# Attention followed by a squared-ReLU MLP on one core: the transpose of one token tile moves from TensorE to a DMA, and the order around it is planned anew

## The chip, the cores and the metric

The kernel runs on one core of one Trainium2 chip. The metric is the device time of one execution in microseconds (us). The kernel before takes 211.44 us, the median of 4 runs (211.15 to 211.97). Smaller is better.

## What is computed

The inputs are q, k and v of shape (4, 8, 768, 64) in float32 (batch, heads, sequence, head size), and two weight matrices, `w_in` (512 x 2048) and `w_out` (2048 x 512). Cut to its core, the reference is:

```
scores = (q @ k.T) / 8 + bias            # per batch and head; bias = -slope[h] * distance
scores = where(keep, scores, -1e9)       # keep: 96 local positions back, and the 8 first ones
a   = softmax(scores)
x   = (a @ v), heads side by side        # 3072 tokens x 512
h   = max(x @ w_in, 0)
out = (h * h) @ w_out                    # 3072 tokens x 512
```

Because only the last 96 positions and the first 8 count, a tile of 128 queries needs the keys and values of its own tile and of the tile before it, plus 8 global positions.

## The kernel before, in words

**Tiles and blocks.** The 3072 tokens are 24 tiles of 128, six to a batch. Two tiles make a block (12 blocks) for the MLP, so tiles 6 and 7 are block 3, tiles 8 and 9 block 4, and so on. Tile 0, 6, 12 and 18 are the first of a batch and have no tile to their left.

**What one tile goes through.** Each step is an operation with a short name; `sc(9)` is the scores of tile 9, `s1(3,0)` the first slice of the first MLP matmul of block 3.

- `load(j)`: POOL starts three DMAs, for q, k and v of the tile, which also turn float32 into bf16 (line 213, called from line 244). q and k go into one of three shared buffers (`qk_6` to `qk_8`), so a load waits until the transposes of the tile three places earlier have read that buffer.
- `T(j)`: q and k are transposed. Tiles 0 to 5 do it on TensorE (`tr`, line 402) with a copy out of PSUM; from tile 6 on (`JQK = 6`) SP starts one transposing DMA (line 426).
- `gate(j)` for tiles 8, 9, 10 (line 376): a tiny DVE write into the q/k buffer, placed in DVE's order so that the load that follows it cannot start before that point.
- `sc(j)`: score matmuls on TensorE into PSUM (line 489); `exp` on ACT (line 555); `mul` by a table of exp(bias) and mask on DVE (line 580).
- `pv(j,0)`, `pv(j,1)`: probabilities times v for four heads each (line 642, tile `po`); `norm` on DVE: a reciprocal (line 669) and a multiplication (line 670) that writes half of `x` of the tile.
- `x` (128 tokens x 512) must be transposed to `xT` before the MLP can use it. For tiles under `JX` TensorE does it: `trx` (line 705), four 128x128 transposes into PSUM, and a copy to SBUF, on ACT (line 330) or DVE (line 332), whichever the planner takes. For tiles from `JX` on, SP starts a transposing DMA (line 729) and nothing else is needed. Before, `JX = 8`.
- `gk`, `gv`, `kl`: small DVE copies that put the 8 global keys and values next to the tile for its right neighbour.

**What one block goes through.** `s1(b,s)`, s = 0 to 7: eight matmuls `xT` x `w_in` into PSUM (line 757, tile `hT`); `relu` on ACT (line 778, `hr`); `sq` on DVE (line 790, `hs`); `s2(b,s,half)`: two matmuls `hs` x `w_out` each for tile 0 and 1 of the block (line 830, `acc`); after the eighth slice `o` copies `acc` to SBUF (ACT or DVE) and `st` stores it (SP, line 872).

**What sets the order.** A planner (class `Plan`) is run when the kernel is built. It holds for each operation its engine, a cost, what it depends on, and a due key; it emits the instructions of every engine in the order in which its model starts them, and on the chip each engine runs its list strictly in that order. The key of tile j's operations comes from `LEADS` (line 178: how much ahead of its block a tile is due) and from `SHIFT` (line 34: a correction for each kind of operation, or for one kind and one tile or block). `STEP` (line 188) ties `sc(j)` behind a certain `s1`; `HOLD` (line 187) lets the next `s1` also wait for that `sc`. `SAFE` and `SAFEX` (lines 179, 180) add time to the model's landing of some transposing DMAs. `JOIN` puts the scores of a tile into one operation with those of the tile before.

**Shared resources.** Six PSUM banks (tag `g`) go round among `tr`, `sc`, `po`, `trx` and `hT`; two belong to `acc`. `xT` has three buffers, `x` two, `hr` two, `hs` fourteen. SP's list holds all transposing DMAs (of q/k and of x) and all stores, in one order; POOL's list holds all loads.

Of the kernel before, what the change touches and what calls it, by code (L numbers as in the profile page):

```python
# [21 lines left out]
class Plan:  # L22
# [8 lines left out]

    LAG = {"PE": 0.25, "ACT": 0.26, "DVE": 0.2, "SP": 0.6, "POOLQ": 0.8, "DMAQ": 1.2, "DMA": 0.0}
    URGE = 0.01
    SHIFT = {'T': 47, 'sc': -5.25, 'pv': -2, 'norm': 26.5, 'trx': -2, 'xT': 51, 'gk': 42, 'gv': -127.5, 'mul': 24, 'kl': 38.5, 'relu': 25.5, 'sq': 30, 's2': -5, 'o': 61, 'st': 78, ('mul', 3): 28, ('tr', 4): 10, ('xT', 5): -22, ('sc', 6): 14, ('pv', 7): -4, ('norm', 7): -17, ('trx', 7): -3, ('sc', 8): -12, ('pv', 8): -18, ('pv', 10): 45, ('sc', 11): 12, ('pv', 12): -50, ('sc', 13): 17, ('sc', 14): 6, ('pv', 14): 10, ('norm', 14): -28, ('sc', 15): -21, ('exp', 15): 20, ('exp', 16): 83, ('mul', 16): 92, ('norm', 16): -9, ('sc', 17): 32, ('pv', 17): 28, ('pv', 21): 9.5, ('pv', 22): -10, ('norm', 22): 8, ('s1', 2): -8.5, ('sq', 2): -10, ('relu', 3): 24, ('sq', 3): -82, ('s1', 5): 6, ('s1', 6): 30, ('sq', 6): 6, ('s1', 7): -6, ('sq', 7): -92, ('relu', 8): 40, ('s1', 9): -2, ('s1', 10): -10, ('s2', 0): 7.5, ('s2', 2): 1, ('s2', 4): -15, ('s2', 5): 37, ('s2', 6): -5, ('s2', 7): -3, ('s2', 9): 4.5, ('s2', 11): 30}

    def shift(self, name):
        early = name[-1 if name[0] in ("T", "tr") else 1]
        return self.SHIFT.get(name[0], 0.0) + self.SHIFT.get((name[0], early), 0.0)

# [65 lines left out]
def kernel(  # L105
# [35 lines left out]
    NFIRST = 4  # L141
    NSPLIT = 4
    NBIAS = 3
    JQK, JX = 6, 8
    NQ, NKT = 3, 2 * TPB
    NG = 8 - NACC
    G = ("g", NG)
# [7 lines left out]
    def const(shape, dt, name):  # L155
        return consts.tile(shape, dt, name=name, tag=name)
# [18 lines left out]
    pbt = const([P, 2, P], FP32, "pbt")  # L175
    pbw = const([P, 2, P], FP32, "pbw")
    plan = Plan()
    LEADS = {3: 51, 4: 17, 5: 16, 6: 27, 8: 2, 9: 20, 10: 42, 11: 47, 12: 0, 14: 0, 15: 7.5, 16: 34, 17: 46, 20: 28, 21: 15, 23: 56}
    SAFE = {j: 1.6 for j in range(6, 12)} | {14: 4.2, 15: 3.2, 16: 3.5}
    SAFEX = {9: 1.5, 11: 1.5, 13: 2.5}  # L180

# [2 lines left out]
    JOIN = {(7, 0), (12, 0), (21, 0), (16, 0), (23, 0), (18, 0), (20, 0), (15, 0)}  # L184
    COPY = [14, 15, 19, 20, 22]
    BEHIND = {}
    HOLD = ((10, 0),)
    STEP = {(4, 0): -7, (12, 0): 37, (5, 0): -2, (10, 0): 29, (13, 0): 30, (23, 1): 81}
    JGATE = 11
    NHS = 14  # L190
    NWARM = 8
# [72 lines left out]
    def emit_ones(e, js):  # L264
        for j in js:
            nc.vector.memset(v_sb[j][:, :, D : D + 1], 1.0)
# [38 lines left out]
    for g in range(NFIRST + 2, NT, 6):  # L305
        js = range(g, min(g + 6, NT))
        o = plan.op(
            ("ones", g), {"DVE": 0.2}, lambda e, js=js: emit_ones(e, js),
            key=-1.0, ready=15.0,
        )  # L310
# [40 lines left out]
    kl = [const([P, NPAIR, P], BF16, f"kl_{i}") for i in range(2 if COPY else 0)]  # L351
# [8 lines left out]
    for j in range(NT):  # L360
        b, t = divmod(j, TPB)
        first = t == 0
        need = 8 * (j // 2)
        base = need - LEADS.get(j, LEAD) + 4 * (j % 2)
        if (j, 0) in JOIN:
# [29 lines left out]
        for n in range(2) if j < JQK else ():  # L395
            users = []

            def emit_tr(e, j=j, n=n, fp=fp):
# [9 lines left out]
            tr = plan.op(  # L408
                ("tr", n, j), {"PE": 0.5 if fp else 0.24}, emit_tr,
                deps=[land["qk"[n], j]], key=base, takes=(*G, [users]),  # L410
            )
# [12 lines left out]
        if j >= JQK:  # L424
            def emit_dT(e, j=j, T_=T_):
# [5 lines left out]
            T = plan.op(  # L431
                ("T", j), {"SP": 1.3}, emit_dT,
                deps=[land["q", j], land["k", j], xT_op[j - 3]] + ku, key=base - 6,
            )
            T = plan.op(("moved", j), {"DMAQ": 1.2}, None, deps=[T])
            qk_users[slot(j)].append(T)
            if j in SAFE:

                T = plan.op(("seen", j), {"DMA": SAFE[j]}, None, deps=[T])
# [6 lines left out]
        mul, mul_users = {}, {}  # L446
# [55 lines left out]
        for gs in SETS.get(j, [tuple(range(groups))]):  # L502
            n = 8 * len(gs)
            sc_users = busers[2 * gs[0] : 2 * gs[-1] + 2]
            if (j, gs[0]) in JOIN:

                o, also, taken = joint
# [16 lines left out]
            if j < NBIAS:  # L524
# [6 lines left out]
            o = plan.op(  # L531
                ("sc", j, gs[0]), {"PE": 0.2 + 0.029 * n},
                lambda e, gs=also, f=emit_sc: f(e, gs), deps=[*deps, bias],
                key=base + 1 + 2 * gs[0], takes=takes,
            )
# [91 lines left out]
        norm = []  # L627
# [170 lines left out]
    for o in plan.ops:  # L798
        if o["name"][0] == "sc":
            j = o["name"][1]  # L800
            n = STEP.get(o["name"][1:], 4 * j - LEAD)
            if n >= 0 and j >= NFIRST:
                o["deps"].append(s1_ops[n // NSTEP, n % NSTEP])
                if o["name"][1:] in HOLD:
                    n += 1
                    s1_ops[n // NSTEP, n % NSTEP]["deps"].append(o)

    for blk in range(NBLK):
# [9 lines left out]
        for s, sub, half in order2:  # L818
# [5 lines left out]
            def emit_s2(e, blk=blk, s=s, sub=sub, half=half, w=w, cols=cols, own=own):  # L824
# [15 lines left out]
            o = plan.op(  # L840
                ("s2", blk, s, sub), {"PE": 0.43 * w / d_model}, emit_s2,
                deps=[d, land["wout", s]] + users[-1:],
                key=8 * blk + s + 2.0 + (0 if not last else 8 * sub + 8 * (half or 0)),
                takes=((*G, [users]) if own else ("acc", NACC, [users])) if s == 0 else None,
            )
# [6 lines left out]
            if s == NSTEP - 1:  # L852
# [14 lines left out]
                def emit_st(e, blk=blk, sub=sub, half=half, cols=cols):  # L867
# [9 lines left out]
                st = plan.op(  # L877
                    ("st", blk, sub), {"SP": 0.8 if (blk, sub) in HALVES else 0.4}, emit_st,
                    deps=[ev, s1_ops[NLATE, 0] if blk < NLATE - 2 else None],
                    key=8 * blk + s + 9.0,  # L880
                )
                st = plan.op(("stored", blk, sub), {"DMAQ": 1.4}, None, deps=[st])
# [40 lines left out]
```

## Time and profile before

| | |
|---|---|
| median of the 4 runs | 211.44 us |
| the profiled execution | 211.66 us |
| its span, first to last instruction | 209.9 us |
| TensorE (PE) busy | 202.5 us, 96% of the span |
| DVE, ACT, POOL busy | 140.9, 120.0, 73.8 us |
| chain that ended last | PE 88%, POOL 5%, DMA 4% |
| `hT` matmuls, L757 | x768 |
| `acc` matmuls, L830 | x373 |
| `trx` transposes, L705 | x32 |
| transposing DMAs of x, L729 | x16 |
| transposing DMAs of q/k, L426 | x18 |

The profile is of one execution. Its own time is 211.66 us, 1.76 us more than its span and 0.22 us over the median of the runs. A group's line gives how many instructions it has, the busy time and the mean of one in ns, and the idle time of the engine just before them. PE is the matmul stream, PEld the loads of its weights, which run beside it. "DMA to landing" is the time from the start of the issue on the queue to the arrival of the data. The stretch up to about 20 us is the start, in which TensorE waits for the first slices of `w_in`; the last 10 us are the second matmul of the last block, its copy and its store.

### The profile page before, as it was taken

How to read it: one execution, taken by the hardware profiler on the slowest of the kernel's cores; microseconds unless marked ns; L12 is line 12 of the kernel's file. 1: busy time of each engine (PE TensorE's matmuls, PEld its weight loads, DVE VectorE, ACT ScalarE, POOL GpSimd, SP SyncE). 2: the span in 40 equal slices, each digit the busy share in tenths (PEclk: the TensorE clock that was granted, in tenths of full speed). 3: DMA queues.
4: the chain of work that ended last, by engine and by line, in shares of the span. 5: the costliest groups of instructions: out<-in, count | busy, mean ns of one | idle time of the engine just before them, and what ended most of it. 6: DMA issues, size and time to landing. Idle time of an engine off the chain costs nothing.

```text
span 209.9 us, 4980 instructions
## 1 busy us (share of the span) xinstructions
PE 202.5 (96%) x1957; PEld 141.8 (68%) x1984; DVE 140.9 (67%) x370; ACT 120.0 (57%) x224; POOL 73.8 (35%) x91
## 2 busy tenths in 40 slices
PE   7997999999999999999999999999999999999994
PEld 3776877666756677676866676776676865865853
DVE  7698698533595878585968666676696865781730
ACT  6785678234772674664737464663575826841631
POOL 8996766431927064413274222222500000000000
PEclk9999999999999999999999999999999999999999
DMA  9999999999999999999999692989983421130402
GB/s 131 152 168 186 184 190 199 177 176 213 139 169 119 196 139 134 213 91 95 214 152 144 177 102 52 133 127 142 197 61 75 123 55 28 54 96 3 102 0 100
DMA packets 112649, 27.32 MB, mean 130 GB/s; under 512 B 103282, under 2 KB 109682, under 8 KB 112626
## 3 DMA queue, kind: packets, MB, share of 16 engines
q0 software_dynamic: 79200, 13.37, 83.9%
q1 hardware_dynamic: 33426, 13.64, 33.1%
q8 instruction: 15, 0.25, 0.5%
q14 instruction: 8, 0.07, 0.1%
HBM read 27.26 MB, written 6.29 MB: 160 GB/s over the span
## 4 chain that ended last, share of the span: by engine, by line
PE 88%; POOL 5%; DMA 4%; issue 1%; DVE 1%; ACT 0%; POOLq 0%
PE acc L830 39%; PE hT L757 39%; PE sc L489 5%; PE po L642 4%; DMA win<-in_moe_w_in_dram 4%; POOL qk L213 3%; POOL v L213 2%; POOL win L213 1%; PE trx L705 1%; PE tr L402 1%; DVE x L670 0%; DVE hs L790 0%; POOL pbi L269 0%; DVE rs L669 0%; ACT o L330 0%
## 5 line engine op out<-in xcount | busy, mean ns | idle before, releaser
L757 PE MATMUL hT<-xT,win 128*128 128x256 bf16 x768 | 93.5, 273 | 1.4 <-DMA win<-in_moe_w_in_dram 1.3
L830 PE MATMUL acc<-wout,hs 128*128 128x512 bf16 (+2 forms) x373 | 87.1, 370 | 1.7 <-issue 0.3
L778 ACT ACTIVATE hr<-hT 128x512 f32<-128x512 f32 x96 | 57.3, 603 | 47.5 <-PE hT L757 42.3
L757 PEld LDWEIGHTS <-win 128*128 128x128 bf16 x768 | 72.8, 98 | 15.7 <-DMA win<-in_moe_w_in_dram 1.9
L790 DVE TENSOR_TENSOR hs<-hr 128x512 bf16<-128x512 f32 x96 | 64.7, 686 | 23.5 <-ACT hr L778 22.8
L830 PEld LDWEIGHTS <-hs 128*128 128x128 bf16 x400 | 36.8, 98 | 33.8
L555 ACT ACTIVATE esc<-sc 128x512 bf16<-128x512 f32 x78 | 39.9, 613 | 12.6 <-PE sc L489 12.6
L213 POOL DMA_DIRECT2D qk<-in_q_dram x23 | 20.6, 898 | 70.1 <-DMA qkT<-qk 54.3
L580 DVE TENSOR_TENSOR at<-esc,E 128x512 bf16<-128x512 bf16 x78 | 32.3, 422 | 10.1 <-ACT esc L555 7.2
L330 ACT COPY o<-acc 128x512 f32<-128x512 f32 (+2 forms) x21 | 11.6, 576 | 19.8 <-PE acc L830 19.8
L213 POOL DMA_DIRECT2D v<-in_v_dram x24 | 21.8, 909 | 2.0 <-DMA win<-in_moe_w_in_dram 1.6
L670 DVE TENSOR_TENSOR x<-po,rs 128x256 bf16<-128x256 f32 x48 | 20.4, 424 | 1.7
L213 POOL DMA_DIRECT2D qk<-in_k_dram x23 | 20.8, 907 | 0.5 <-DMA win<-in_moe_w_in_dram 0.5
L642 PEld LDWEIGHTS <-at 128*128 128x128 bf16 x352 | 15.7, 98 | 4.5
L642 PE MATMUL po<-v,at 128*128 128x65 bf16 x352 | 17.3, 193 | 0.0
L669 DVE RECIPROCAL rs<-po 128x4 f32<-128x4 f32 x48 | 8.5, 177 | 11.3 <-PE po L642 10.8
L489 PEld LDWEIGHTS <-qkT 64*128 64x128 bf16 x312 | 9.4, 94 | 5.7 <-issue 4.9
L489 PE MATMUL sc<-qkT 64*128 64x128 bf16 x192 | 12.6, 218 | 0.0
L489 PE MATMUL sc<-qkT,qkT 64*128 64x128 bf16 x120 | 8.5, 216 | 0.0
L332 DVE COPY o<-acc 128x512 f32<-128x512 f32 x4 | 2.8, 692 | 6.2 <-PE acc L830 6.2
L213 POOL DMA_DIRECT2D win<-in_moe_w_in_dram x8 | 6.1, 778 | 1.4 <-issue 0.7
L213 POOL DMA_DIRECT2D wout<-in_moe_w_out_dram x8 | 5.7, 713 | 1.9 <-DMA win<-in_moe_w_in_dram 1.1
(45 smaller groups left out, 68.6 us busy)
## 6 DMA issues: line engine op xcount, KB each, us to landing
out_dram<-o SPq DMA_DIRECT2D x21, 256.0 KB, 3.0
v<-in_v_dram POOLq DMA_DIRECT2D x24, 128.0 KB, 5.6
qk<-in_q_dram POOLq DMA_DIRECT2D x23, 128.0 KB, 4.5
qk<-in_k_dram POOLq DMA_DIRECT2D x23, 128.0 KB, 5.2
win<-in_moe_w_in_dram POOLq DMA_DIRECT2D x8, 256.0 KB, 8.2
wout<-in_moe_w_out_dram POOLq DMA_DIRECT2D x8, 256.0 KB, 9.3
out_dram<-o SPq DMA_DIRECT2D x4, 128.0 KB, 2.4
qkT<-qk SPq DMA_TRANSPOSE x18, 5.3
```

What stands on the lines that cost most here:

```text
L213: nc.gpsimd.dma_start(out=dst, in_=src)
L330: nc.scalar.copy(dst, src)
L489: nc.tensor.matmul(out=tiles["sc", j, odd, g][:, at, :], lhsT=left[j - 1][half, pair, :] if kt else qkT[j % NKT][half, 1, pair, :], rhs=qk ...
L555: nc.scalar.activation(out=esc, in_=tiles.pop(("sc", j, odd, g)).rearrange("p a c -> p (a c)"), func=Act.Exp, scale=scale,)
L580: nc.vector.tensor_mul(at, tiles.pop(("esc", j, odd, g)), bias)
L642: nc.tensor.matmul(out=po[:, hi, :], lhsT=tiles["at", j, odd, g][:, at * P : (at + 1) * P], rhs=v_sb[kj][:, h, :], start=(i == 0), stop=(i ...
L669: nc.vector.reciprocal(rs, po[:, :, D : D + 1])
L670: nc.vector.tensor_tensor(out=x[:, 4 * hf : 4 * hf + 4, :], in0=po[:, :, :D], in1=rs.to_broadcast([P, 4, D]), op=Alu.mult,)
L757: nc.tensor.matmul(out=hT[:, c, :], lhsT=w_in_sb[s][:, kt, c * P : (c + 1) * P], rhs=tiles["xT", blk][:, kt, :], start=(kt == 0), stop=(kt ...
L778: nc.scalar.activation(hr, tiles.pop(("hT", blk, s)), Act.Relu)
L790: nc.vector.tensor_mul(hs, hr, hr)
L830: nc.tensor.matmul(out=tiles["acc", blk, sub, half], lhsT=hs[:, c, sub * P : (sub + 1) * P], rhs=w_out_sb[s][:, c, cols], start=(s == 0 an ...
```

## The change

`JX` goes from 8 to 7: `x` of tile 7 is transposed by a DMA that SP starts, like the tiles after it, and no longer by TensorE. The four `trx(7)` transposes and the copy `xT(7)` leave; one transposing DMA `xT(7)` joins SP's list. `HOLD` becomes empty and the `STEP` of tile 10 leaves, that of tile 13 goes from 30 to 32. `LEADS` of tiles 5 to 15 and of tile 23 and most of `SHIFT` have new values, so the planner's order changes on every engine but POOL.

```
-    JQK, JX = 6, 8
+    JQK, JX = 6, 7
-    LEADS = {3: 51, 4: 17, 5: 16, 6: 27, 8: 2, 9: 20, 10: 42, 11: 47, 12: 0, 14: 0, 15: 7.5, 16: 34, 17: 46, 20: 28, 21: 15, 23: 56}
+    LEADS = {3: 51, 4: 17, 6: 40, 7: 16, 8: 20, 9: 50, 10: -43, 12: -11, 13: -1, 14: -38, 15: 28, 16: 34, 17: 46, 20: 28, 21: 15}
-    HOLD = ((10, 0),)
-    STEP = {(4, 0): -7, (12, 0): 37, (5, 0): -2, (10, 0): 29, (13, 0): 30, (23, 1): 81}
+    HOLD = ()
+    STEP = {(4, 0): -7, (12, 0): 37, (5, 0): -2, (13, 0): 32, (23, 1): 81}
-    SHIFT = {'T': 47, 'sc': -5.25, 'pv': -2, 'norm': 26.5, 'trx': -2, 'xT': 51, 'gk': 42, 'gv': -127.5,
...
+    SHIFT = {'T': 47, 'sc': -6, 'exp': -12, 'pv': -2, 'norm': 32, 'trx': -17, 'xT': 43.5, 'gk': 57,
...
```

What this does to the built order: POOL's list is the same. On SP the new `xT(7)` stands between the store of block 1's second tile and `T(9)`; `T(6)` goes ahead of the first store, and some later stores change places with transposes. On TensorE the four `trx(7)` transposes are gone, `sc(8)` follows seven `s2` steps of block 2 instead of three and `trx(7)`, `sc(10)` and `sc(13)` now stand between `s2` steps (before, `sc(10)` followed `s1(3,7)` and `sc(13)` stood between `s1(4,7)` and `s1(5,0)`), and many single `s1`, `s2` and `pv` steps change places by one or two. The copies of `xT(3)` and `xT(4)` go from ACT to DVE, that of `xT(0)` from DVE to ACT; seven of the `o` copies are on DVE, where four were.

More of the change, by code (lines that the diff above doesn't have):

```diff
@@ L33 @@
     URGE = 0.01
-    SHIFT = {'T': 47, 'sc': -5.25, 'pv': -2, 'norm': 26.5, 'trx': -2, 'xT': 51, 'gk': 42, 'gv': -127.5, 'mul': 24, 'kl': 38.5, 'relu': 25.5, 'sq': 30, 's2': -5, 'o': 61, 'st': 78, ('mul', 3): 28, ('tr', 4): 10, ('xT', 5): -22, ('sc', 6): 14, ('pv', 7): -4, ('norm', 7): -17, ('trx', 7): -3, ('sc', 8): -12, ('pv', 8): -18, ('pv', 10): 45, ('sc', 11): 12, ('pv', 12): -50, ('sc', 13): 17, ('sc', 14): 6, ('pv', 14): 10, ('norm', 14): -28, ('sc', 15): -21, ('exp', 15): 20, ('exp', 16): 83, ('mul', 16): 92, ('norm', 16): -9, ('sc', 17): 32, ('pv', 17): 28, ('pv', 21): 9.5, ('pv', 22): -10, ('norm', 22): 8, ('s1', 2): -8.5, ('sq', 2): -10, ('relu', 3): 24, ('sq', 3): -82, ('s1', 5): 6, ('s1', 6): 30, ('sq', 6): 6, ('s1', 7): -6, ('sq', 7): -92, ('relu', 8): 40, ('s1', 9): -2, ('s1', 10): -10, ('s2', 0): 7.5, ('s2', 2): 1, ('s2', 4): -15, ('s2', 5): 37, ('s2', 6): -5, ('s2', 7): -3, ('s2', 9): 4.5, ('s2', 11): 30}
+    SHIFT = {'T': 47, 'sc': -6, 'exp': -12, 'pv': -2, 'norm': 32, 'trx': -17, 'xT': 43.5, 'gk': 57, 'mul': 27.5, 'kl': 67.5, 'relu': 22, 'sq': 58, 's2': -5, 'o': 43, 'st': 118, ('mul', 3): 28, ('tr', 4): 10, ('tr', 5): -24, ('pv', 5): -2, ('exp', 6): -11, ('exp', 7): -34.5, ('pv', 9): 30, ('sc', 10): -33, ('pv', 10): -40, ('sc', 13): 11, ('mul', 13): -20, ('sc', 14): -8, ('pv', 14): -24, ('sc', 15): -6, ('pv', 15): -36, ('norm', 15): 46, ('exp', 16): 83, ('mul', 16): 92, ('sc', 17): 32, ('pv', 17): 28, ('pv', 21): 10, ('pv', 22): -10, ('s1', 2): -8.5, ('s1', 4): 19.5, ('relu', 4): 84, ('s1', 5): 24, ('s1', 6): 34, ('sq', 6): 21, ('s1', 7): -7, ('relu', 8): 40, ('s1', 9): -2, ('s1', 10): -10, ('s2', 0): 7.5, ('s2', 2): 1, ('s2', 3): 22, ('s2', 4): 25, ('s2', 5): 42, ('o', 5): 30, ('s2', 6): -23, ('s2', 7): -3, ('s2', 9): 4.5, ('s2', 11): 30}
     def shift(self, name):
```

## The prediction

> **What bounds the kernel now.** I read the page first (busy shares, the slices, the share of the chain), then the chain of waits around tile 7, then what touches the tiles `trx` and `xT`, then the DMA queues in two short windows.
>
> The page, its busy line, and its PE and DMA slices:
>
> ```profile
> PE 202.5 (96%) x1957; PEld 141.8 (68%) x1984; DVE 140.9 (67%) x370; ACT 120.0 (57%) x224; POOL 73.8 (35%) x91
> ...
> DMA  9999999999999999999999692989983421130402
> ...
> PE 88%; POOL 5%; DMA 4%; issue 1%; DVE 1%; ACT 0%; POOLq 0%
> ```
>
> TensorE is the bound: the chain is PE from about 20 us to the end. The windows view from 20.5 to 193 us:
>
> ```profile
> 20.50:193.00 172.50, 170.71 (x1633) 118.95 (x1658) 118.00 (x281) 99.68 (x184) 55.65 (x65) 1.00 1.21 133
> ```
>
> PE is idle for 172.50 - 170.71 = 1.8 us there, in scraps; the granted clock is 1.00. So a gain comes from work taken off TensorE, and a loss from anything that makes it wait. The second thing to see is the DMA row: some queue has work until about 115 us (22 of 40 slices), and the new transfer joins it there. The chain around tile 7 (start, length):
>
> ```profile
> 58.91 0.24 PE po L642 x8
> 59.16 1.29 PE acc L830 x6
> 60.45 0.22 PE trx L705 x4
> 60.68 0.55 PE sc L489 x16
> ...
> 66.57 2.62 PE hT L757 x24
> ```
>
> The `po` piece is `pv(7,1)`, which finishes tile 7; `trx(7)` costs 0.22 us on the path, and block 3, which needs `xT(7)`, starts at 66.57.
>
> **The change, part by part.**
>
> *Removed on TensorE.* Four transposes: -0.22 us by the row above, on the path.
>
> *Removed on ACT.* One copy:
>
> ```profile
> L330 ACT COPY xT<-trx x5: 577/585/585, 18.1 to 60.7; 128x512 bf16<-128x512 bf16 x5
> ...
> L729 SPq DMA_TRANSPOSE xT<-x x16: 1188/1190/1749, 65.6 to 184.6; - x16
> ...
> DMA to landing us min/median/max: 2.4/2.7/6.9
> ```
>
> 0.58 us of an engine that is 57% busy: 0, covered by TensorE's own work. A PSUM bank is also freed, and no wait for banks shows on PE here: 0.
>
> *Added: the wait for a DMA.* Before, 66.57 - 58.91 = 7.66 us lie between `pv(7,1)` and block 3. After, `trx(7)` is gone (-0.22) and one more `s2` step stands there (+0.43, half of the 0.86 that four `acc` matmuls take): 7.87 us. The second half of `x(7)` was ready at 60.07 (the DVE row at 59.65 that lasts 0.42), 1.16 after `pv(7,1)` began, and SP follows 0.07 later (for tile 8: ready at 65.52, issued at 65.59). That leaves 7.87 - 1.23 = 6.6 us for issue and landing. The rows give 2.4 to 6.9, so this wait costs from 0 to +0.3. I take 0, because of what is in flight, which the DMA view shows in two windows, 61.4 to 63.6 and 64 to 68 us:
>
> ```profile
> q1 hardware_dynamic: 817, 0.23, 75.7%
> q0 software_dynamic: 69, 0.01, 6.2%
> ```
>
> ```profile
> q0 software_dynamic: 4040, 0.51, 200.0%
> ...
> q1 hardware_dynamic: 8, 0.00, 0.4%
> ```
>
> q1 carries SP's DMAs, q0 POOL's loads. Between the load that was issued until 57.8 and the one issued from 61.79 there is a gap in which SP's queue runs alone; from 64 on the load's packets hold SP's queue still (8 packets of 4049, with `xT(8)` issued at 65.59 and landed 6.2 later). `xT(7)` is issued at about 59.6, so it starts in the gap: with the 2.4 of a free one from the end of the load (61.4) it lands by 63.8 at the latest, 2 us early.
>
> Here the Trainium skill says otherwise in two places. DMA: Bandwidth & Descriptors (Queues, rings and completion order) has each DMA engine serve its queues in turn, packet by packet; by that SP's queue would have had near half of the packets from 64 to 68, not 8 of 4049; the gap would not matter, the sum would stay at -0.22 and a late start would cost next to nothing. The trace speaks against it here. VectorE: DVE Perf Modes (Rules for kernel authors) advises TensorE for a 128x128 transpose where the result may go to PSUM, which speaks against this change; by it the sum would be 0 or more. The row of 0.22 us on a bound TensorE against a transfer with 2 us to spare says the opposite.
>
> *What `xT(7)` pushes on SP.* It stands before `T(9)`, which was issued at 58.78 and now starts after the 1.19 us issue, at about 61.0; free, a `T` lands 3.1 after its start (the one at 51.54), so 64.1, against the load's packets from about 64. Even if it lost 5 us there, `sc(9)` (69.19 before, later by 0.6 in the new order) still has its data: 0. `T(10)` and `T(11)` go by `xT(8)` and two stores and move by about the same 1 us as the `sc(10)` that uses them (landed at 74.5, used at 76.42): 0, at most +0.3 if it takes 7.2 (the longest `T`) instead of 6.5.
>
> *POOL.* The list is the same. The load of tile 10 waits for `gate(10)`, which stays behind `sq(2,7)`; DVE reaches it some 0.4 us later, since the multiplication and `norm` of tile 7 come first. Landing has seconds to spare: 0. The load of tile 12 needs `T(9)` to have read its buffer: 0 to 4 us later for a `T(12)` that landed at 82.9 and is used at 86.67: 0.
>
> *Positions of the scores.* `sc(10)` and `sc(13)` now stand among `acc`. The weight loads are idle 0.21 before scores that follow `hT` (76.35) and 0.42 where they follow `acc` (86.60), but scores that are followed by `hT` pay a step as well. From below and above: -0.2 to +0.2 for all of them; I take 0, since one is between `hT` before and one is not.
>
> *Other moves.* Copies of `xT(3)`, `xT(4)` and three `o` go to DVE (0.42 and 0.69 each). `sq(0,0)` waits for `xT(3)`, so it starts at about 21.0 instead of 19.34; its reader `s2(0,0)` starts at 23.4. Cover 1.7 us; if that is gone, `relu(0,2)` and the PSUM banks behind it come late next. `mul(7,1,1)` now follows both `norm(6)`: done at about 58.1 for a `pv(7,1)` at 58.2. Cover 0.1; if gone, +0.1 to 0.3. Steps of tiles 4 and 5 may save 0.1, but that stretch is paced by weight slices that land just before their use, so 0. Bounds for all of these: -0.1 to +0.5; I take 0, because the rows before had equally thin covers and no wait.
>
> *Sum.* -0.22 against the profiled execution's own 211.66 (span 209.9 and 1.76 around): 211.44. That execution lies 0.22 over the median of the runs, so 211.2 for the median. No term reaches 0.3% (0.63 us), about what a measurement of this kernel can tell from no change.
>
> **The rivals.**
>
> *Slower, `xT(7)` misses the gap.* If its packets come after the load's (q0, from about 64.2), it waits until that load has landed: issued at 63.52 + 0.4, 5.2 to landing, so 69.1, for a block 3 that is due at 65.9: +3.2, 214.4. It decides where `xT(7)` would have landed later than 64.2, 4.6 after its issue; half lost, a landing at 67, costs +1.1. For it: `xT(8)`, `xT(12)` and one more took over 6 us. Against it: `gate(10)` holds the load behind `norm(7)` on DVE by construction.
>
> *`xT(11)` meets the load of tile 16.* Before, it was issued at 91.79 and landed in 2.4, just ahead of a load from 93.42; `xT(12)`, 4 us on, took 6.9. From `pv(11,1)` to block 5 are 7.3 us in both orders, 1.2 of them until the issue. At 6.9 it is 0.8 late: 212.0. It needs the load to start 1.1 us earlier against `xT(11)`, through a `T(13)` that now goes out about 1 us earlier on SP.
>
> *The gain is eaten by small waits* of DVE and ACT, as above: +0.2 to +0.5, 211.4 to 211.7.
>
> *Faster by more.* The reorder also removes part of the 1.8 us of scraps: a third of them gives 210.6. Against: most follow scores, and there are as many scores as before.
>
> *That the change does not do what it says* is excluded by the built lists: 28 `trx` weight loads for 32, and one more transposing DMA.
>
> **How the numbers follow.** Forecast, 211.2: 0.38. Small waits: 0.15. `xT(11)` late: 0.16, half of it over 212.07. `xT(7)`, or a `T` behind it, late by 1 to 3 us: 0.23. Faster by more: 0.08. So faster 0.08, same 0.38 + 0.15 + 0.08 = 0.61, slower 0.08 + 0.23 = 0.31. The range goes from 210.7 (half of the last case below it) to 213.0 (about half of the late `xT(7)` above it); the forecast's own range is 210.9 to 211.6.
>
> **What the profile after would show.** `trx` x28. Right: `xT(7)` issued near 59.6 and landed before 64; block 3's first `hT` near 65.9 with no wait before it; PE idle between 20.5 and 193 still about 1.8 us; all later steps 0.1 to 0.3 us earlier. Wrong: a gap on PE before an `hT`, `sc` or `po` group with a DMA or DVE as its releaser, above all at 66, 77, 87 or 98 us. What would upset it all is a start that moves: the first 20 us wait for `w_in`, and nothing here is meant to touch them.

## The result and the profile after

The changed kernel takes 212.15 us in the median (211.02 to 213.63), beside 211.38 us of the kernel before in the same comparison: 1.0029 of its time, 95% interval 1.0017 to 1.0041. It is slower by some 0.6 us by that ratio, and by 0.77 us between the two medians. The forecast was 211.2; the time lies inside the range (210.7 to 213.0), but the kernel moved to the slower side, which had got a chance of 31%.

The profiled execution took 212.53 us (span 210.8). Its page, in the same rows as before: busy times, the DMA slices, and the chain by engine and by line.

```profile
PE 202.3 (96%) x1953; PEld 141.0 (67%) x1980; DVE 145.3 (69%) x375; ACT 118.0 (56%) x218; POOL 73.9 (35%) x91
...
DMA  9999999999999999999999679999993421301402
...
PE 84%; DMA 8%; DVE 5%; issue 1%; SPq 0%; ACT 0%
PE hT L757 37%; PE acc L830 36%; DMA xT<-x 6%; PE sc L489 5%; PE po L642 4%; DMA plain<-in_k_dram 2%; DVE x L670 1%; PE tr L402 1%; PE trx L705 1%; DVE E L338 1%; DVE rs L669 1%; DVE qkT L616 0%; PE sc L469 0%; DVE E L339 0%; DVE qkT L332 0
```

TensorE's share of the chain fell from 88% to 84%, and 6% of the chain are now transposing DMAs of x. Around tile 7 the chain (start, length) is as it was meant to be: no `trx` after the `po` that is `pv(7,1)` (the `trx` row is tile 6), and `hT` of block 3 follows `acc` at 65.43 with no DMA between.

```profile
57.34 0.22 PE trx L705 x4
57.57 0.24 PE po L642 x8
...
58.08 2.75 PE acc L830 x12
...
65.00 0.43 PE acc L830 x2
65.43 0.66 PE hT L757 x6
```

The waits of TensorE name the loss (us in total, times, longest):

```profile
PE hT L757 <- DMA xT<-x: 1.2, 2, 0.9
```

The kernel before has no such row. The chain from 120 to 150 us, where TensorE alone stood before, shows where the two are:

```profile
122.78 0.71 PE acc L830 x4
123.49 6.10 DMA xT<-x
129.59 0.05 issue
129.64 3.67 PE hT L757 x32
...
139.70 6.47 DMA xT<-x
146.18 0.05 issue
146.22 3.67 PE hT L757 x32
```

These are `xT(15)`, for which block 7 waits, and `xT(17)`, for which block 8 waits. Each took over 6 us from issue to landing. The reason stands in the lists of SP and POOL. The timeline of SP and of POOL in the kernel before:

```profile
115.86 1.25 SPq L426 DMA_TRANSPOSE qkT<-qk  x1
117.87 0.81 SPq L872 DMA_DIRECT2D out_dram<-o  x2
123.70 1.19 SPq L729 DMA_TRANSPOSE xT<-x  x1
```

```profile
119.45 0.88 POOL L213 DMA_DIRECT2D qk<-in_q_dram  x1 [6.72 <-DMA qkT<-qk]
```

And in the changed kernel:

```profile
117.54 0.87 SPq L872 DMA_DIRECT2D out_dram<-o  x2
118.52 1.29 SPq L426 DMA_TRANSPOSE qkT<-qk  x1
123.49 1.66 SPq L729 DMA_TRANSPOSE xT<-x  x1
```

```profile
122.29 0.88 POOL L213 DMA_DIRECT2D qk<-in_q_dram  x1 [11.22 <-DMA qkT<-qk]
```

`T(17)` (the `qkT<-qk` row) now stands behind the two stores of block 5. It frees the buffer into which the load of tile 20 goes (the bracket: POOL sat idle until a `qkT<-qk` DMA), so this load starts 2.84 us later, at 122.29, 1.2 us ahead of `xT(15)`. Near 139 us it is the other way round: `T(19)` landed at 136.93 instead of 140.03, so the load of tile 22 started at 137.46 instead of 140.56, 2.2 us ahead of `xT(17)` instead of 0.2 behind it. The rows of POOL for this load and of SP for `xT(17)`, before and after:

```profile
140.33 1.20 SPq L729 DMA_TRANSPOSE xT<-x  x1
140.56 0.88 POOL L213 DMA_DIRECT2D qk<-in_q_dram  x1 [8.17 <-DMA qkT<-qk]
```

```profile
137.46 0.88 POOL L213 DMA_DIRECT2D qk<-in_q_dram  x1 [3.14 <-DMA qkT<-qk]
139.70 1.20 SPq L729 DMA_TRANSPOSE xT<-x  x1
```

A measure that leaves the start aside is the time from the first `hT` of block 1 to the end of TensorE's work, worked out from the start times of the steps (a step is counted from the load of its first weights): 185.80 us before, 187.18 after. From the first step of block 6 to that of block 8 it is 34.36 us after; without the two waits it would be 32.79, as the runs below show. So 1.57 us are lost there, and the rest of the kernel is 0.2 us shorter than before.

### The profile page after: what moved, and what is told of

Its sections match the earlier page's. It is cut to its first block, busy times and chain, and to the rows that moved or that the text cites. A ratio compares the mean times of both kernels' runs of the same rounds, so it can differ in the third digit from the quotient of the medians.

```text
span 210.8 us, 4966 instructions
## 1 busy us (share of the span) xinstructions
PE 202.3 (96%) x1953; PEld 141.0 (67%) x1980; DVE 145.3 (69%) x375; ACT 118.0 (56%) x218; POOL 73.9 (35%) x91
## 4 chain that ended last, share of the span: by engine, by line
PE 84%; DMA 8%; DVE 5%; issue 1%; SPq 0%; ACT 0%
PE hT L757 37%; PE acc L830 36%; DMA xT<-x 6%; PE sc L489 5%; PE po L642 4%; DMA plain<-in_k_dram 2%; DVE x L670 1%; PE tr L402 1%; PE trx L705 1%; DVE E L338 1%; DVE rs L669 1%; DVE qkT L616 0%; PE sc L469 0%; DVE E L339 0%; DVE qkT L332 0%
## 5 line engine op out<-in xcount | busy, mean ns | idle before, releaser
L330 ACT COPY o<-acc 128x512 f32<-128x512 f32 (+2 forms) x18 | 10.0, 563 | 20.1 <-PE acc L830 18.4
L332 DVE COPY o<-acc 128x512 f32<-128x512 f32 x7 | 4.8, 682 | 4.9 <-PE acc L830 4.8
```

Source lines behind the costliest of these rows:

```text
L330: nc.scalar.copy(dst, src)
```

## The experiments

The theories were these. **A**: the loss is the late landing of `xT(15)` and `xT(17)`, beside the loads of tiles 20 and 22. **B**: the transposition of tile 7 by DMA itself costs the time. **C** and **D**: the start does. Later came **E** and **G**: `T(10)`, beside the load of tile 12, loses time as well. **F** and **H**: the loss is spread and sits in none of these places. "Block 1 to the end" and "block 6 to block 8" are the two measures from above, each from one profiled execution; ratios are against the kernel before on the same chip, with the 95% interval.

### Holding a load until the transpose has gone out

The planned order is kept as a list, and a load is moved behind a chosen step of VectorE. A small memset on the load's buffer makes POOL wait for that step:

```
+    def hold(j, behind):
+        load = order.pop(find("load", j))
+        def emit_hold(e):
+            nc.vector.memset(qk_ring[slot(j)][:, :, :1], 0.0)
+        at = find(*behind) + 1
+        order[at:at] = [dict(engine="DVE", emit=emit_hold, name=("hold", j)), load]
+    hold(20, behind=("norm", 15, 1))
+    hold(22, behind=("norm", 17, 1))
```

The run with one load held has only the last line. The fourth run has, in place of the hold of tile 20, `T(17)` moved ahead of `st(5,0)` in the list.

The changed kernel again:

> The changed kernel once more, as the base of the three runs beside it. Theory A (the loss is two late landings: xT(15) meets the load of tile 20 and xT(17) meets the load of tile 22): 212.1, and its profile again has a wait of 0.4 to 1.2 us before the first hT of block 7 (near 129 us) and of block 8 (near 145 us), with a DMA xT<-x as releaser. Theory B (the transposition of tile 7 by DMA, or the new order of TensorE's steps, costs the time everywhere): 212.1, with the loss spread over many small waits and no single one over 0.3 us. Theory C (the start differs, since the slices of w_in land at other times): between 211.3 and 212.1, and the loss in the profile lies before 21 us.

The load of tile 22 held:

> The changed kernel, with the load of tile 22 held by a small memset on VectorE until norm(17,1) is done, so that xT(17) is issued ahead of it; 0.1 us of VectorE work is added. Theory A: xT(17) lands about 3.6 us after its issue, as in the kernel before (140.33 to 143.94), instead of 6.47; the wait of 1.1 us before block 8 is gone, the wait before block 7 stays: 1.1 us less where the stall is there, so 211.1 to 211.5 for the median. Theory B: no change, 212.1. Theory C: no change, 212.1.

Both held:

> As the run before, and the load of tile 20 is held likewise until norm(15,1) is done, so that xT(15) is issued ahead of it (the load would start at 123.6 instead of 122.29). Theory A: neither block 7 nor block 8 waits for xT; 1.1 + 0.45 = 1.55 us less in the profiled execution, 0.8 to 1.3 us less in the median: 210.8 to 211.3, so at or below the kernel before by the 0.22 of the removed transposes. Theory B: 212.1. Theory C: 212.1.

`T(17)` ahead of the stores, tile 22 held:

> The changed kernel with the load of tile 22 held as above, and with T(17) moved on SP ahead of the two stores of block 5, where the kernel before has it; the load of tile 20 is not held. Theory A: T(17) is issued near 116.5 instead of 118.52, qk buffer comes free 2 us earlier, the load of tile 20 starts near 120 instead of 122.29 and xT(15) is less late: the wait before block 7 falls from 0.45 to at most 0.2 us; 210.9 to 211.4, 0.2 to 0.5 under the run with the load of tile 22 alone held. If it is not the load of tile 20 that delays xT(15), the wait before block 7 stays. Theory B: 212.1.

In the last two columns are the us by which the load's issue starts ahead of the transpose's (negative: behind it), and the us from the transpose's issue to its landing.

| kernel | ratio | block 1 to the end | block 6 to block 8 | `xT(15)`: load ahead by, landed after | `xT(17)`: the same |
|---|---|---|---|---|---|
| changed again | 1.0030 (1.0002 to 1.0058) | 187.64 | 33.61 | 1.2, 6.5 | 2.9, 3.9 |
| tile 22 held | 1.0053 (1.0027 to 1.0078) | 185.88 | 33.10 | 1.2, 5.9 | -0.3, 3.7 |
| tiles 20 and 22 held | 1.0014 (0.9978 to 1.0050) | 185.57 | 32.79 | -0.3, 4.2 | -0.3, 3.7 |
| `T(17)` ahead, 22 held | 1.0034 (1.0009 to 1.0060) | 186.23 | 33.46 | 3.3, 5.0 | -1.5, 3.0 |

In the profiles theory A did what it said: where the load goes out behind the transpose, the transpose lands in about 4 us and the wait is gone. The chain with both loads held, at the places where the waits were:

```profile
130.15 0.86 PE acc L830 x4
131.02 3.49 PE hT L757 x32
...
146.40 0.12 PE po L642 x4
146.52 3.49 PE hT L757 x32
```

In the fourth run `xT(15)` is in time by 0.5 us, as expected, but `po` of tile 18 waited 0.5 us. The hold itself did that: VectorE's memset must wait until `T(19)` has read the buffer, `T(19)` took 8.5 us here and landed at 141.56, and the multiplication behind the memset came late. In VectorE's timeline:

```profile
141.72 0.42 DVE L580 TENSOR_TENSOR at<-esc,E 128x512 bf16<-128x512 bf16 x1 [1.10 <-DMA qkT<-qk]
141.72 0.06 DVE L898 MEMSET qk<- 128x2 bf16 x1
```

The times were a miss for theory A. With both loads held the median was 212.18 us, where 210.8 to 211.3 was expected (the kernel before took 211.77 on this chip, the changed one 212.24); with `T(17)` ahead it was 212.38 against 210.9 to 211.4; and the run with tile 22 held, at 212.84, was no faster than the changed kernel at all. Its profile spent its time in the start, where the first `hT` came at 17.57 us instead of 15.2, behind a first k tile that landed at 6.65 instead of 5.34. With twelve timed runs each, the spread between executions was as large as what was looked for. So the mechanism was shown, and not yet what it weighs.

### The parts of the change, one at a time

`trx(7)` out of the kernel before and a transposing DMA in its place:

```
+    order.pop(find("trx", 7))
+    order[find("xT", 7)] = dict(engine="SP", emit=by_dma, name=("xT", 7))
```

(`by_dma` starts the DMA of line 729 for tile 7.) The next three take the order of all engines from one kernel up to a step and from the other behind it (the start ends at the first step of block 1, the middle at the first step of block 6). The runs of the late part as before and of the middle alone have six timed executions each.

> The kernel before with one thing changed: trx(7) and its copy on ScalarE are left out, and xT(7) is written by a transposing DMA on SP, behind T(9); every other step keeps its place. Theory B (the transposition by DMA itself costs time, because block 3 waits for it): 0.3 us or more over the kernel before, with a wait before the first hT of block 3. Theory A (the loss is late landings of xT(15) and xT(17), made by the new order of the late steps) and theory D (the new order of the first 20 us makes the chain up to block 0 some 0.5 us longer): 0.22 us under the kernel before, no wait before block 3.

(The expectation puts `xT(7)` behind `T(9)`. In the run it took the place of the copy that it replaces, which is ahead of `T(9)`: it was issued at 59.96 us, `T(9)` at 61.26.)

> The changed kernel up to the first step of block 6 (about 112 us), and from there on every engine's steps in the order of the kernel before, so that T(17) stands ahead of the stores of block 5 again. Theory A: no wait before blocks 7 and 8; block 1 to the end takes 185.6 us as in the run with both loads held, and the median is 0.2 us under the kernel before (ratio 0.999), 0.5 to 0.8 under the changed kernel. Theory D: the median stays 0.2 to 0.6 over the kernel before, since the start is the changed one. Theory B: 0.6 over it.

> Only the middle of the changed kernel: up to the first step of block 1 (about 20 us) and from the first step of block 6 (about 112 us) the order is that of the kernel before; between them it is the changed one, with the transposition of tile 7 by DMA and the leads of tiles 5 to 15. Theory A and theory D: 0.2 us under the kernel before (ratio 0.999). Theory B, or the new order of tiles 5 to 15 as a cause: 0.3 to 0.6 us over it, with waits between 20 and 112 us.

> The converse: the kernel before up to the first step of block 6, x of tile 7 transposed by TensorE, and from there on the order of the changed kernel. Theory A: the load of tile 20 goes out some 3 us later and meets xT(15): a wait of 0.4 to 1.2 us before block 7 or block 8 in the profile, and 0.3 to 1.0 us over the kernel before. Theories B and D: as the kernel before, within 0.2 us.

| kernel | ratio | block 1 to the end | waits of TensorE in its profile, net |
|---|---|---|---|
| DMA for tile 7 alone | 1.0019 (1.0002 to 1.0037) | 185.57 | none after block 1 |
| late part as before | 1.0038 (1.0026 to 1.0050) | 186.68 | 0.44 before `s1(0,4)`, 0.15 at `sc(6)` |
| middle alone | 1.0054 (1.0034 to 1.0073) | 187.18 | 1.06 at `sc(10)` |
| late part alone | 1.0031 (1.0002 to 1.0059) | 186.75 | before `s1(7,0)` and `s1(8,0)`, together near 1 |

The late part alone does what theory A says: put into the kernel before, it brings the wait row that this kernel did not have.

```profile
PE hT L757 <- DMA xT<-x: 0.6, 2, 0.4
```

With the late part as before, blocks 7 and 8 do not wait, as theory A expected, but the median is 0.4% over the kernel before, a miss. Of its 1.1 us over 185.57, 0.6 are the waits of the table (the first is for a slice of `w_in`), and 0.5 lie between blocks 6 and 8, where the two orders are joined, in no wait over 0.2 us.

And the middle alone costs as much as the late part: 1.06 us at one place, beside 0.93 for the two waits of the late part. (Another 0.5 us of its 187.18 lie at the same join as in the row above, so its ratio overstates the middle.) Theory A had no place for that. Its chain (start, length) shows another transposing DMA, `T(10)`, for which `sc(10)` waits:

```profile
68.81 9.24 DMA qkT<-qk
78.05 0.05 issue
78.10 0.62 PE sc L489 x16
```

The transposition by DMA alone is the part that theory B blames. Its profile has no wait before block 3, and from block 1 to the end it is exactly 0.23 us shorter than the kernel before (185.57 for 185.80), which is what the four transposes cost. Its median is not lower, though. In its profile `xT(9)` lands 0.30 us before its use, where the kernel before had 2.39: `xT(7)` ahead of `T(9)` moves `T(9)` from 58.78 to 61.26, the load of tile 12, whose buffer `T(9)` frees, from 64.4 to 67.5, and the transposes behind it meet other loads. That this is what kept the median up is not shown by one profile, in which nothing was late.

### The place of `xT(7)` on SP

`xT(7)` behind `T(9)` instead of ahead of it, in the kernel with the DMA alone and in the changed kernel with both loads held:

```
+    move(("T", 9), ahead=("xT", 7))
```

> As the run with the transposition of tile 7 alone, but xT(7) stands behind T(9) on SP instead of ahead of it. Theory E (xT(7) ahead of T(9) delays T(9) by 1.1 to 2.5 us; T(9) frees the buffer of the load of tile 12, which goes out 1.4 to 3 us later, and T(10) and xT(9), which run beside that load and the next, land with less slack or late): T(9) is issued near 58.8 again, the load of tile 12 starts near 64.4 instead of 67.5, T(10) lands near 74.5 with 1.8 us to spare, xT(9) has some 2.4 us to spare instead of 0.30; the median is 0.2 us under the kernel before (ratio 0.999). Theory B (the transposition by DMA itself costs time): still 0.1 to 0.5 us over the kernel before, with a wait before block 3 where xT(7) lands after 65.8.

> The kernel before once more, for the spread between runs of one and the same kernel: ratio 1.000, within 0.2%. Theory A and theory E: in its profile T(10) lands at least 1 us and xT(15), xT(17) at least 1.5 us before their use, and TensorE waits for no xT or qkT. If one of these is late here too, the margins of the kernel before are no better than those of the changed one, and both theories fall.

> The transposition of tile 7 by DMA alone, ahead of T(9), once more, beside the run with the other place of xT(7). Theory E: the load of tile 12 again starts 2 to 3 us later than in the kernel before, and xT(9) or T(10) lands with less than 1 us to spare or late; 0.2 to 0.5 us over the kernel before in the median, and 0.3 to 0.7 over the run in which xT(7) stands behind T(9).

> The changed kernel with all three places mended: xT(7) behind T(9) on SP, and the loads of tiles 20 and 22 held until norm(15,1) and norm(17,1), so that xT(15) and xT(17) are issued ahead of them. Theories A and E together: no wait for xT or qkT on TensorE in the profile, block 1 to the end takes 185.6 us, and the median is 0.2 us under the kernel before (ratio 0.998 to 1.000). Theory D (the start's chain is longer by 0.5 us): 0.1 to 0.4 us over the kernel before in spite of that.

| kernel | ratio | block 1 to the end | to spare: `T(10)`, `xT(9)`, `xT(7)` |
|---|---|---|---|
| DMA alone, behind `T(9)` | 0.9994 (0.9969 to 1.0020) | 185.70 | 0.28, 2.02, late |
| before again | 1.0008 (0.9981 to 1.0034) | 185.80 | 0.95, 2.77, - |
| DMA alone, ahead of `T(9)` | 1.0008 (0.9986 to 1.0030) | 186.06 | 2.80, 0.65, in time |
| changed, `xT(7)` behind `T(9)`, loads held | 1.0011 (0.9988 to 1.0035) | 185.76 | 0.79, 3.99, late |

Behind `T(9)`, `xT(7)` takes 5.9 us (the profile's rows for this DMA) and block 3 waits for it, 0.13 us net (185.70 for 185.57), and 0.19 in the changed kernel (185.76):

```profile
L895 SPq DMA_TRANSPOSE xT<-x x1: 2642/2642/2642, 60.1 to 60.1; - x1
...
DMA to landing us min/median/max: 5.9/5.9/5.9
```

That was a miss: theory E expected `T(10)` to gain from this place, and it had 0.28 us to spare, less than before. So by these margins `xT(7)` ahead of `T(9)` is the better of the two, and it was in time there in every profile. Of the 0.49 us that the run with `xT(7)` ahead lies over 185.57, 0.33 are at `acc` and a slice of `w_out` near 36 us, and none at a transpose. The second profile of the kernel before has the same 185.80 us and no wait for a transposed tile. The times of the four can't be told apart.

### How much of the loss of the median the two landings are

The changed kernel and the one with both loads held, twice each on one chip:

> The changed kernel again, as one of two repeats beside two repeats of it with both loads held. Theory A (the late landings of xT(15) and xT(17) make most of the loss of the median): 0.2 to 0.4% over the kernel before; a wait before block 7 or 8 in the profile. Theory F (the loss of the median is spread over landings of the whole kernel, the start and T(10) too): the same here.

> The changed kernel with the loads of tiles 20 and 22 held, again. Theory A: no wait before blocks 7 and 8, and 0.3 to 0.5% (0.6 to 1.0 us) under the changed kernel of the same call, so 0.1% under to 0.1% over the kernel before. Theory F: no wait there either, but only 0 to 0.2% under the changed kernel, and still 0.1 to 0.3% over the kernel before.

> The changed kernel, second repeat of this call: theory A and theory F both 0.2 to 0.4% over the kernel before; the profile tells how often the waits before blocks 7 and 8 come back.

> Both loads held, second repeat of this call. Theory A: 0.1% under to 0.1% over the kernel before. Theory F: 0.1 to 0.3% over it.

| kernel | ratio | block 1 to the end | block 6 to block 8 |
|---|---|---|---|
| changed | 1.0099 (1.0073 to 1.0126) | 187.48 | 34.71 |
| changed | 1.0079 (1.0048 to 1.0110) | 187.70 | 33.72 |
| both loads held | 1.0017 (0.9993 to 1.0042) | 185.96 | 32.79 |
| both loads held | 1.0028 (1.0013 to 1.0043) | 185.62 | 32.80 |

Here the intervals are apart. The two holds take back 0.5 to 0.8% (1.1 to 1.7 us) of the 0.8 to 1.0% that the changed kernel loses on this chip. All four profiles of the changed kernel have a wait for `xT(15)`, three of the four also one for `xT(17)`; the chain of the first one here:

```profile
124.08 6.71 DMA xT<-x
...
140.91 6.22 DMA xT<-x
```

Theory A holds for most of the loss. But 0.2 to 0.3% are left, as theory F had it, although the steps are shorter. In the third row's profile `sc(10)` waited 0.38 us for `T(10)`; the fourth row's profile has no such wait.

### Holding the load beside `T(10)` too

```
+    hold(12, behind=("sq", 3, 1))
     hold(20, behind=("norm", 15, 1))
     hold(22, behind=("norm", 17, 1))
```

> The changed kernel with three loads held: those of tiles 20 and 22 as before, and that of tile 12 until sq(3,1) is done on VectorE (about 68.6 us), so that T(10), issued near 68.1, goes ahead of it. Theory G (what is left of the loss, 0.2 to 0.3% with the two loads held, comes from T(10) beside the load of tile 12): T(10) lands after 5 to 6 us instead of 7 to 9, has 2 us or more to spare, and the median is 0.3 to 0.5 us under the run beside it, at 0.999 to 1.001 of the kernel before. Theory H (it comes from elsewhere, the start and the first 40 us above all): T(10) may land earlier, but the median stays where it is beside the other run; if T(12) is late by the hold, above it.

> The changed kernel with the loads of tiles 20 and 22 held, beside the run with three loads held, on the same chip. Theory G and theory H both: 1.001 to 1.003 of the kernel before, no wait before blocks 7 and 8, T(10) with 0 to 1.2 us to spare.

With three loads held the ratio is 0.9983 (0.9964 to 1.0002), with two 1.0029 (1.0000 to 1.0058). The profile's rows for `T(10)` with three loads held, and the chain at the same place with two:

```profile
L426 SPq DMA_TRANSPOSE qkT<-qk x1: 1288/1288/1288, 69.4 to 69.4; - x1
...
DMA to landing us min/median/max: 4.0/4.0/4.0
```

```profile
46.76 7.61 DMA qkT<-qk
54.37 0.05 issue
54.41 0.62 PE sc L489 x16
...
70.77 9.05 DMA qkT<-qk
79.82 0.05 issue
79.87 0.23 PE sc L489
```

`T(10)` lands in 4.0 us, with 4.4 to spare, instead of 9.05 and late, and block 1 to the end takes 185.57 us again, the 185.80 of the kernel before less 0.23. Theory G fits: this kernel is no longer slower than the kernel before. That it is faster is not shown, since the interval reaches 1.0002, and what `T(10)` weighs is not measured well: the intervals of the two runs touch, and the profile with two loads held is of the slowest of its 12 executions (214.27 us, the median 212.13). The third hold also moves what comes behind it: in its profile the load of tile 16 starts 1.2 us ahead of `xT(11)`, which takes 5.6 us, `xT(9)` takes 6.9, and each lands only 0.4 to 0.5 us before the first `hT` that needs it. The second fence shows one more place in the run with two loads held: `T(7)` took 7.61 us, and `sc(6)`, which is joined with `sc(7)`, waited 0.93 us net. Four of the 13 profiles with the changed start and middle have this wait (0.15 to 1.13 us), none of those with the start and middle of the kernel before. In the changed order a store stands between `T(6)` and `T(7)` on SP; that this is the cause was not tried.

## Why the prediction was wrong

**Right: the sum for TensorE.** `trx(7)` was costed at -0.22 us, its copy and the steps moved among each other at 0. Measured without waits: 185.57 us for 185.80, -0.23, in the run with the DMA alone, in the first of those with two loads held and in the one with three.

**Right: `xT(7)` in time.** It was issued at 58.55 and block 3 did not wait. The rival that has it miss the gap did not come in that place. But the margin of 2 us was too well thought of: it rested on the 2.4 us of a free transfer, and 0.2 us later on SP, behind `T(9)`, the transfer took 5.9 us and was late. And the row of 8 packets of 4049 says less than was read from it: its window opens at 64, while `xT(8)` was issued at 65.59. The last section counts from a better point.

**Wrong: "Other moves" and "POOL".** The failed step is that moves on SP were followed only up to tile 13, and that the loads, whose list had not changed, were costed at 0. The list was the same, but each load waits for the transpose that frees its buffer. `T(17)` behind two stores stood in the built order and in no term of the sum. It made the load of tile 20 start 2.84 us later, so that it went from 4.2 us to 1.2 us ahead of `xT(15)`; `T(19)`, which landed earlier, made the load of tile 22 start 3.1 us earlier, 2.2 us ahead of `xT(17)` instead of 0.2 us behind it. The two waits cost 1.57 us in the profile of the changed kernel. A row that tells of such a price was there before: `xT(12)` had taken 6.9 us, issued 2.2 us behind the start of a load.

**Right mechanism, wrong place: the rival of `xT(11)`.** "A transposing DMA meets POOL's load" was named, with 6.9 us for it, but for tile 11 alone. `xT(11)` landed in 2.9 us in the changed kernel. The same question, put for every block with the moves of SP followed to the loads, would have come to tiles 15 and 17.

**Mis-sized: `T(10)`.** "0, at most +0.3 if it takes 7.2" became 7 to 9.2 us, and waits of up to 1.06 us in the profiles that have the changed middle. For the load of tile 12 the prediction asked only whether `T(12)` would still be early enough, not what runs beside that load. (The "seconds to spare" of its POOL paragraph are microseconds.)

**Did not come: small waits of DVE and ACT.** After block 1 the profile of the changed kernel has none over 0.2 us.

**Open.** The changed order's start: block 1 begins at 21.27 us in the mean of 13 profiles with the changed start (20.35 to 22.57) and at 21.08 in 7 with the start of the kernel before (20.83 to 21.31). It hangs on the landing of the slices of `w_in` and the first k tile, which the change does not touch, and no run here tells whether the 0.2 us are more than chance. Nor is it known why the changed kernel loses 0.3% on some chips and 0.8 to 1.0% on another.

## What to carry to other kernels

When a load waits for the step that frees its buffer, an unchanged list of loads does not mean unchanged loads: follow each moved transpose to the buffer it frees, to the load that starts then, and to what that load runs beside, through the whole kernel and not only around the edit. On a bound engine it is the time to spare of each DMA that an order should be compared by, and one small wait that sends a load out behind the transfer that is needed sooner can be worth more than the work that was taken off the engine.

## What the runs showed that was not expected

In these profiles a transposing DMA's time depends on how far POOL's load is ahead of it, and not in one direction. From all 20 profiles, where the landing is recorded (start of the load's issue before that of the transpose; issue to landing):

| DMA | load behind it or up to 0.2 ahead | 0.4 to 2.8 ahead | 2.9 or more ahead |
|---|---|---|---|
| `xT(15)`, load of tile 20 | 4.1 to 5.3 us | 5.5 to 6.7 us | 4.2 to 5.0 us |
| `xT(17)`, load of tile 22 | 3.0 to 4.4 us | 5.1 to 6.5 us | 3.9 us (one profile) |
| `T(10)`, load of tile 12 | 4.0 to 5.0 us (three profiles) | 7.4 to 9.2 us | 6.5 to 8.2 us |

It is slow when it comes just behind the start of a load. A transpose that goes first, even by 0.3 us, is done in 3.0 to 5.3 us, and one that comes 3 us behind the load is faster again, `T(10)` only by a little.

The packets show where most of the time goes. In the kernel before, `xT(17)` went out just ahead of the load: issued at 140.33 us, it had no packet until 141.5, and from there its packets took 0.9 us. The DMA view from 141.5 to 142.4 us:

```profile
q1 hardware_dynamic: 512, 0.13, 74.1%
```

In the changed kernel it was issued at 139.70, so that after the same 1.2 us its packets were due from 140.9. From there to 143 us the view gives POOL's queue (q0) and SP's (q1):

```profile
q0 software_dynamic: 1587, 0.20, 152.8%
q1 hardware_dynamic: 268, 0.07, 37.5%
```

SP's queue got 268 of 1855 packets (14%), none of them before 141.7, and its 512th went at about 143.9, if the packets of `T(20)`, issued on the same queue at 141.02, came behind. So some 2.2 of the 2.9 us by which `xT(17)` took longer lie before its last packet.

The Trainium skill, DMA: Bandwidth & Descriptors (Queues, rings and completion order), has each DMA engine take turns between its queues packet by packet. With turns of equal size, SP's queue would have had near half of the packets. The page's packet holds several descriptors, typically 9 to 17; how many of the profile's packets make one such turn is not shown here, so an uneven share need not go against the rule, but half does not come out of it either. The window of the prediction, begun where the packets of `xT(8)` were due (65.59 + 1.2), gives the same 14%; from 66.8 to 69 us in the kernel before:

```profile
q0 software_dynamic: 1866, 0.24, 182.0%
q1 hardware_dynamic: 303, 0.08, 43.2%
```

The measured share decides. Why the load comes before is not shown by any run.

TensorE itself repeats to a few hundredths: block 1 to the end takes 185.80 us in both profiles of the kernel before and 185.57 in three different kernels without `trx(7)`. What differs between the profiles of one kernel is the start (block 1 begins between 20.35 and 22.57 us over all of them) and waits, for late landings above all.
